# Attention of batches 1 to 7 with the key-value blocks as stationary operand, sums of squares by products with ones, and factors spread through DRAM

## The chip, the cores and the metric

The kernel runs on one core of a Trainium2 chip. The metric is the time of one execution on the device, in microseconds (us). Three runs of the kernel before gave 1651.33, 1654.06 and 1650.82, so the median is 1651.33. All traces are of single profiled executions.

Five engines work side by side, each in the order of its own instructions: PE multiplies matrices (a stationary operand is loaded, a moving one streams past it, the product lands in a bank of PSUM), DVE and ACT work on elements and are the ones that empty PSUM here, POOL does element work in SBUF, SP issues DMAs. They wait for one another by semaphores.

## What is computed

The reference, cut to what matters. All numbers are float32.

```python
# q, k, v: (8 batches, 8 heads, 576 tokens, 64)
kv  = np.einsum('bhsd,bhse->bhde', k, v)
out = np.einsum('bhsd,bhde->bhse', q, kv)
rms = np.sqrt(np.mean(out * out, axis=-1, keepdims=True) + 1e-06)
x   = out / rms * g_norm                 # then heads side by side: x is (4608, 512)
p   = domain_probs / (domain_probs.sum(-1, keepdims=True) + 1e-09)
for e in range(4):                       # w1[e]: 512 x 1024, w2[e]: 1024 x 512
    out += p[:, e:e + 1] * (np.maximum(x @ w1[e], 0.0) @ w2[e])
```

There is no softmax: a head's keys and values shrink to one 64 x 64 block `kv`, and each token's row of q is multiplied by it. The row of 64 that results is divided by its root mean square. The second part multiplies x (and the hidden layer) by the weights of four experts; it is most of the arithmetic.

## The kernel before

**The two parts.** The tokens come in nine chunks of 512: chunk c below 8 is the first 512 tokens of batch c, the ninth holds the last 64 tokens of all batches (`REM`). For every expert e and chunk c there is one step s = 9e + c of products up and down. These use a scheme with seven products for eight blocks at two levels, so their operands are sums and differences of blocks, which DVE and POOL make (`x_forms`, `combine`), and their results are added by DVE (`total` in `up`, line 1370). A product is issued by `halves_of` (line 479) as two halves of 64 columns of the array.

**Attention of batches 1 to 7** (`attention`, lines 956 to 1168) runs beside the products of expert 0: batch c + 1 in step c. It makes x in turned form, features on partitions and tokens along the row, because a product needs x that way. Per batch there are two halves s of four heads (two pairs o, two heads r each):

- q is loaded by eight DMAs and turned in blocks of 32 by DVE (line 1035).
- `key_values`: 20 products make the four 64 x 64 blocks; ACT copies them to SBUF.
- `attend`: blocks of 64 tokens of q are stationary and a 64 x 64 block of kv moves past them, 32 products for the first 512 tokens (line 1088) and 4 for the last 64 (line 1097). The results have tokens on partitions.
- `evacuate` copies them to SBUF. `norm_rows` squares on ACT (line 995), sums over the 64 features on DVE (line 1001), takes the square root on ACT and inverts it with one refining step on 16 columns (`inverse_root`, lines 720 to 739), and multiplies x by the factors (line 1010).
- `turn_x` (line 1129) turns x by eight transposes on PE, and ACT copies them out of PSUM times the gain (line 1138).

The last 64 tokens of both halves are normed together at the end of the batch, turned by two transposes (`turn_left`, line 1150), copied (line 1156) and stored in DRAM in `x_left`.

Batch 0 goes another way (`opening`), which the change leaves alone.

**What sets the order.** Nothing of it is written by hand. `plan.add` takes each operation with a key (its place in steps), a cost in us for each engine that may do it, what it reads and writes, and `kb` for a DMA. `Plan.layout` then lays out the whole program before it is issued: an engine that comes free takes the ready operation that is due first; PE takes the first ready one in the order of keys. A DMA is booked as ending at `max(bus, t + 1.5) + kb / 215 + 0.5`. `port=True` keeps DVE and POOL from working at once on operations that would share a port. For each step, `layout` tries 12 draws (60 for the early steps) of random shifts of the due times, runs the plan a step and 1.3 further, and keeps the draw that leaves PE idle least. The order of each engine is then fixed in the program; on the chip each instruction still waits by semaphores for what it needs.

**PSUM.** There are eight banks: two each of `u1`, `u2` (products up), `db` (products down) and `ab` (products down and attention). A seed is a copy by ACT into a bank on which PE then adds (`op.seed`); it has to lie on columns that PE wrote last, which the loop at the end (lines 1851 to 1857) asserts from `op.marks`.

Of the kernel before, what the change touches and what calls it, by code (L numbers as in the profile page):

```python
# [27 lines left out]
class Op:  # L28
    def __init__(self, key, cost, fn, reads, writes, kb, port):
        self.key, self.cost, self.fn, self.kb, self.port = key, cost, fn, kb, port  # L30
        self.outs = list(writes)
        self.bufs = list(dict.fromkeys(list(reads) + self.outs))
        self.deps = {}
        self.start = self.end = self.eng = None
        self.marks = self.seed = None
        self.early = self.gang = self.opens = False
# [5 lines left out]
class Plan:  # L42
# [18 lines left out]
    TRIES, LOOK, SPREAD = 12, 1.3, 1.5  # L61
# [32 lines left out]
    def layout(self, slots, later, idle, idle_banks, idle_until):  # L94
# [54 lines left out]
        self.order = []  # L149

        steps = {}
        for op in self.ops:
            steps.setdefault(math.floor(op.key), []).append(op)
        for step in sorted(steps):
            begin = self.save()
            tried = []
            for n in range(self.TRIES * (5 if step < 3 else 1)):
                draw = random.Random(100 * n + step)
                for op in steps[step] + steps.get(step + 1, []):
                    op.due = op.base + (draw.gauss(0.0, self.SPREAD) if n else 0.0)  # L160
                if self.run(step + 1 + self.LOOK):
                    tried.append((self.t - self.worked, n))
                self.restore(begin)
            n = min(tried)[1]
            draw = random.Random(100 * n + step)
            for op in steps[step] + steps.get(step + 1, []):
                op.due = op.base + (draw.gauss(0.0, self.SPREAD) if n else 0.0)
# [6 lines left out]
    def save(self):  # L174
# [4 lines left out]
        copied.update({name: dict(getattr(self, name)) for name in ("live", "ended", "missing", "busy")})  # L179
# [31 lines left out]
    def ready(self, op, eng, front):  # L211
# [10 lines left out]
        for k, n in need.items():  # L222
# [7 lines left out]
            if k in self.first and any(o.due < op.due for o in self.first[k] if o is not op):  # L230
                return None
            when = max(when, sorted(free)[n - 1][0])
# [77 lines left out]
    def begin(self, op, eng):  # L310
# [16 lines left out]
        for b in op.outs:  # L327
            if b.kind is not None and b.slot is None:
                free[b.kind].sort()
                b.slot = free[b.kind].pop(0)[1]  # L330
                b.ap = self.slots[b.kind][b.slot]
        for held in list(self.waiting.values()) + list(self.first.values()):
# [27 lines left out]
def kernel(  # L360
# [60 lines left out]
    gcol = const.tile([P, 1], F32, name="gcol")  # L421
    p_all = const.tile([P, NBLK, E], F32, name="p_all")
# [6 lines left out]
        "ss": (2, 2 * H), "rt": (2, 4 * H),  # L429
# [39 lines left out]
    }  # L469
    plan = Plan()  # L470
# [249 lines left out]
    def inverse_root(key, ss, rt, n, count):  # L720
# [7 lines left out]
        def invert(eng):  # L728
            a, r, w = ss.ap[0:n, 0:count], rt.ap[0:n, 0:count], rt.ap[0:n, 2 * H:2 * H + count]
# [226 lines left out]
    def attention(b, key, span, rem):  # L956
# [25 lines left out]
        def norm_rows(key, name, x, squares, count):  # L982

            ss, rt = Buf("ss", f"ss{name}"), Buf("rt", f"rt{name}")
            width = count * D

            def by_head(ap):
                return ap.rearrange("p (b d) -> p b d", d=D)

            for at_ in range(0, width, NT):  # L990
                n = min(width, NT)
                sq = squares or Buf("ab", f"sq{name}_{at_}")
                plan.add(
                    key, act(n),
                    lambda eng, sq=sq, at_=at_, n=n: nc.scalar.activation(
                        out=sq.ap[:, 0:n], in_=x.ap[:, at_:at_ + n], func=ACT.Square),
                    reads=[x], writes=[sq],
                )
                plan.add(
                    key, dve(n),  # L1000
# [892 lines left out]
```

## Time and profile before

| | before |
|---|---|
| median of three runs | 1651.33 us |
| the profiled execution: span from first to last instruction | 1650.8 us |
| PE busy | 1642.3 us, 99% |
| DVE, ACT, POOL busy | 1255.2, 992.5, 737.0 us |
| moved by DMA | 232.48 MB, 141 GB/s mean |
| TensorE clock granted | 0.999 of full speed |

A row of a group names the line, the engine, the operation, what it writes and reads, the shape and the count; then its busy time in us, the mean of one in ns, and the time that the engine stood idle before it, with what ended most of that. A product on PE appears as two MATMUL records, a transpose as one. Records of PE overlap, so what one costs is read from the distance of starts and not from its length. A row of the view of one line or tile has the shortest, median and longest duration in ns. In the order of time, rows of the same kind are merged: start, length, line, count.

### The profile page before, as it was taken

What the parts mean: (1) busy time and instruction counts of PE and PEld (TensorE: products, weight loads), DVE (VectorE), ACT (ScalarE), POOL (GpSimd) and SP (SyncE); (2) the same over time, 40 slices, a digit from 0 to 9 for tenths busy, and PEclk for the clock granted to TensorE, in tenths of its full rate; (3) what the DMA queues carried; (4) which work ended last, traced back from release to release, by engine and by line L of the source; (5) the groups of instructions that cost most, each with busy time, mean ns of one, the idle gap of its engine ahead of it and who ended that gap; (6) DMA issues with size and microseconds to landing.
All of it is one profiled execution on the core that took longest, in us unless ns stands there. A gap on an engine that the chain in (4) does not pass through costs nothing.

```text
span 1650.8 us, 67181 instructions
## 1 busy us (share of the span) xinstructions
PE 1642.3 (99%) x29226; PEld 1566.0 (95%) x29226; DVE 1255.2 (76%) x2198; ACT 992.5 (60%) x2485; POOL 737.0 (45%) x714
## 2 busy tenths in 40 slices
PE   9999999999999999999999999999999999999998
PEld 5688898888999999999999999999999999999996
DVE  4777867777888777887787787777778877777764
ACT  3555665555566666666666666666666566666662
POOL 4545555453443444444354554443354445433341
PEclk9999999999999999999999999999999999999999
DMA  9867556524566444444557444444577544444442
GB/s 235 221 166 212 162 169 173 174 89 148 187 178 158 109 112 124 136 117 116 156 153 183 117 108 116 115 116 115 132 195 164 136 112 117 117 111 111 117 104 52
DMA packets 202704, 232.48 MB, mean 141 GB/s; under 512 B 92778, under 2 KB 142378, under 8 KB 202410
## 3 DMA queue, kind: packets, MB, share of 16 engines
q1 hardware_dynamic: 178858, 191.41, 37.9%
q0 software_dynamic: 23552, 36.78, 14.9%
q8 instruction: 229, 3.75, 0.9%
q14 instruction: 65, 0.53, 0.1%
HBM read 153.95 MB, written 74.19 MB: 138 GB/s over the span
## 4 chain that ended last, share of the span: by engine, by line
PE 99%; DVE 0%; ACT 0%; issue 0%; DMA 0%; POOL 0%; POOLq 0%
PE u L479 48%; PE db L479 32%; PE ab L479 15%; PE ab L1061 1%; PE ab L1088 1%; PE ab L1129 1%; PE ab L1841 0%; PE u L841 0%; PE db L1097 0%; DMA small<-in_q_dram 0%; PE db L880 0%; PE ab L1150 0%; PE ab L900 0%; PE ab L826 0%; DVE small L1035 0%
## 5 line engine op out<-in xcount | busy, mean ns | idle before, releaser
L479 PE MATMUL u<-xf,big 128*64 128x128 f32 x7072 | 513.3, 273 | 0.0
L502 DVE TENSOR_TENSOR big<-big,big 128x1024 f32<-128x1024 f32 (+1 forms) x482 | 448.4, 947 | 26.4 <-ACT big L1326 12.7
L479 PEld LDWEIGHTS u<-xf,big 128*64 128x64 f32 x7072 | 411.6, 137 | 2.7 <-issue 0.8
L479 PE MATMUL db<-big,big 128*64 128x128 f32 (+1 forms) x5144 | 400.2, 292 | 0.4 <-ACT snap L1683 0.4
L479 PE MATMUL u<-xf,w1y 128*64 128x128 f32 x5304 | 396.0, 273 | 0.0
L479 PEld LDWEIGHTS db<-big,big 128*64 128x64 f32 x5144 | 307.3, 137 | 27.8 <-issue 0.8
L1370 DVE TENSOR_TENSOR big<-u,snap 128x256 f32<-128x256 f32 x460 | 192.8, 421 | 176.4 <-PE u L479 130.1
L502 POOL TENSOR_TENSOR big<-big,big 128x256 f32<-128x256 f32 (+1 forms) x176 | 229.6, 1307 | 193.3 <-DVE big L502 98.9
L479 PEld LDWEIGHTS u<-xf,w1y 128*64 128x64 f32 x5304 | 310.7, 137 | 3.0 <-issue 0.5
L1362 ACT ACTIVATE snap<-u 128x256 f32<-128x256 f32 x490 | 187.2, 382 | 174.7 <-PE u L479 146.1
L1362 ACT ACTIVATE big<-u 128x256 f32<-128x256 f32 x460 | 175.4, 383 | 70.3 <-PE u L479 47.2
L502 POOL TENSOR_TENSOR big<-big 128x512 f32<-128x512 f32 (+1 forms) x89 | 109.4, 1230 | 157.6 <-DVE big L502 107.8
L1683 ACT ACTIVATE snap<-db 128x256 f32<-128x256 f32 x252 | 89.0, 353 | 132.4 <-PE db L479 117.8
L1326 ACT ACTIVATE big<-big 128x1024 f32<-128x1024 f32 x128 | 134.5, 1051 | 4.1 <-DVE big L502 2.4
L1691 DVE TENSOR_TENSOR big<-ab,snap 128x256 f32<-128x256 f32 x162 | 68.3, 422 | 66.6 <-ACT snap L1683 39.5
L1534 POOL DMA_DIRECT2D out_dram<-big x116 | 102.7, 1120 | 35.2 <-ACT big L1510 32.2
L1362 ACT ACTIVATE u<-u 128x256 f32<-128x256 f32 x245 | 90.8, 371 | 38.9 <-PE u L479 26.4
L502 DVE TENSOR_TENSOR big<-big 128x512 f32<-128x512 f32 (+1 forms) x125 | 90.2, 728 | 1.4 <-PE db L479 1.4
L479 PE MATMUL ab<-kv,big 128*64 128x128 f32 x1280 | 89.9, 273 | 0.0
L479 PE MATMUL ab<-big,big 128*64 128x128 f32 (+1 forms) x1256 | 89.8, 277 | 0.0
L1510 ACT ACTIVATE big<-big,p_all 128x256 f32<-128x256 f32 x182 | 85.6, 500 | 1.5 <-DVE big L1721 0.7
L1721 POOL TENSOR_TENSOR big<-big 128x512 f32<-128x512 f32 x22 | 28.1, 1278 | 110.1 <-DVE big L502 97.8
(201 smaller groups left out, 2409.4 us busy)
## 6 DMA issues: line engine op xcount, KB each, us to landing
xf<-x SPq DMA_DIRECT2D x104, 512.0 KB, 3.6
xf<-x_h SPq DMA_DIRECT2D x85, 256.0 KB, 3.3
out_dram<-big POOLq DMA_DIRECT2D x80, 256.0 KB, 5.6
xf<-x SPq DMA_DIRECT2D x78, 256.0 KB, 3.6
x<-xf SPq DMA_DIRECT2D x36, 512.0 KB, 3.6
big<-in_moe_w_dram SPq DMA_DIRECT2D x29, 512.0 KB, 7.3
big<-in_moe_w_dram POOLq DMA_DIRECT2D x18, 512.0 KB, 6.2
x_h<-big SPq DMA_DIRECT2D x17, 512.0 KB, 4.8
```

The lines of the kernel that those rows point to most:

```text
L479: nc.tensor.matmul(out_[cols], lhsT=lhsT[:, cols], rhs=rhs, **kw)
L502: lambda eng: adder(eng).tensor_tensor(out=out_(), in0=a(), in1=b(), op=op),
L1061: nc.tensor.matmul(bank.ap[r * D:(r + 1) * D, o * D:(o + 1) * D], lhsT=ks[r], rhs=vs[r], start=(j == 0), stop=(j == len(sets) - 1), skip_g ...
L1088: nc.tensor.matmul(raw[r].ap[c * D:(c + 1) * D, (o * NR + t) * D:(o * NR + t + 1) * D], lhsT=qt.ap[half, col:col + D], rhs=kv.ap[half, o * ...
L1326: lambda eng: nc.scalar.activation(out=b.ap[:], in_=b.ap[:], func=ACT.Relu),
L1362: lambda eng: nc.scalar.activation(out=where(), in_=ps.ap[:, 0:HN], func=ACT.Copy),
L1370: lambda eng: nc.vector.tensor_tensor(out=block(whole, a, t), in0=src.ap[:, 0:HN], in1=add_.ap[:], op=ALU.add),
L1510: lambda eng: nc.scalar.activation(out=cell(i, half), in_=ap(), func=ACT.Copy, scale=prob()),
L1534: nc.gpsimd.dma_start(out=dst, in_=cell(i)[parts, :], accum_op=ALU.add)
L1683: lambda eng: nc.scalar.activation(out=where(), in_=group_of(ps.ap), func=ACT.Copy),
L1691: lambda eng: nc.vector.tensor_tensor(out=cell(tq, dq), in0=group_of(src.ap), in1=group_of(add_.ap), op=ALU.add,),
L1721: lambda eng: adder(eng).tensor_tensor(out=whole(to), in0=whole(a), in1=whole(b), op=ALU.add),
```

## The change

In `attention`, for each half of a batch:

- **q's layout.** The heads of a pair o now lie on one half of the partitions, the head r along the row. The key-value blocks are placed to match, with `key_values` in another order of loops and the same 20 products.
- **`attend`.** A block of kv is stationary and q streams past it: four products of 320 tokens and four of 256. The result has features on partitions and tokens along the row, so x is turned from the start. `turn_x`, `turn_left` and their copies go, and `norm_rows` with them.
- **Sums of squares.** ACT squares x into what will be x's place. `total` multiplies the squares by `ones`, stationary operands of 32 columns that hold ones for one head each: eight products of 128 columns and four of 32, in four strips of 32 partitions of one bank. So each head's sum over its 64 features stands in a row.
- **The factors.** Root and inversion work on 160 columns (`root`, `invert`, the same refining step). A DMA stores the rows that matter in DRAM (`roots`), two DMAs (`spread`) bring each head's factors back on all 64 partitions of its features, and two more do so for the last 64 tokens (`spread_left`). DVE then multiplies x, gain and factors in one instruction, and in a second for the last tokens.
- The last tokens of a batch are stored in `x_left` from there.

In the planner, the draws of each step are no longer tried but written down (`DEALS`, with a spread of 1, 2 or 4 by the draw's number), also for the steps after attention. `written` tells how many columns of a bank PE wrote last, and a seed (`wants`) takes a bank with enough of them. `sides`, which holds the ones, is set by three memsets on POOL.

The diff, cut to its core:

```diff
-    TRIES, LOOK, SPREAD = 12, 1.3, 1.5
+    SPREADS = 1.0, 2.0, 4.0
+    DEALS = {
+        -2: 25, -1: 39, 0: 49, 1: 28, 2: 72, 3: 8, 5: 18, 6: 22, 7: 12, 8: 22, 9: 17, 10: 9, 11: 22, 12: 28,
+        13: 4, 14: 5, 17: 5, 18: 3, 19: 1, 20: 5, 21: 4, 26: 4, 27: 4, 28: 1, 29: 2, 35: 2
+    }
...
+    def deal(self, step, n):
+
+        draw = random.Random(100 * n + step)
+        for op in self.steps[step] + self.steps.get(step + 1, []):
+            op.due = op.base + (draw.gauss(0.0, self.SPREADS[n % 3]) if n else 0.0)
...
+            if op.wants:
+                free = [f for f in free if self.written.get((k, f[1]), 0) >= op.wants]
+                if not free:
+                    return None
...
+    sides = const.tile([P, 48], F32, name="sides")
+    ones = [sides[:, 16:48], sides[:, 0:32]]
...
             def key_values(eng, bank=kbank, held=held):
+                sets = [list(zip(rows_of(kt), rows_of(vt))) for kt, vt in held]
+                for j in range(len(sets[0])):
+                    for r in range(2):
+                        for o in range(2):
+                            ks, vs = sets[o][j]
                             nc.tensor.matmul(
+                                bank.ap[o * D:(o + 1) * D, r * D:(r + 1) * D],
+                                lhsT=ks[r], rhs=vs[r], start=(j == r == 0),
+                                stop=(j == len(sets[0]) - 1), skip_group_check=True,
                             )
...
+            def attend(eng, raw=raw, rest=rest, kv=kv, qt=qt):
+                for at_, width, to in ((0, FIRST, raw), (FIRST, S - FIRST, rest)):
+                    for r in range(2):
+                        for o in range(2):
+                            half, cols = slice(o * D, (o + 1) * D), slice(r * D, (r + 1) * D)
+                            nc.tensor.matmul(
+                                to[o].ap[cols, 0:width], lhsT=kv.ap[half, cols],
+                                rhs=qt.ap[half, r * S + at_:r * S + at_ + width],
+                            )
+            plan.add(
+                at(2 * s + 1.0), {"PE": 1.1}, attend, reads=[qt, kv], writes=raw + rest,
+                early=True, gang=True,
+            ).wide = {**{b: FIRST for b in raw}, **{b: S - FIRST for b in rest}}
...
+            plan.add(
+                when, act(2 * NT),
+                lambda eng, qt=qt, xh=xh: nc.scalar.activation(
+                    out=two(xh.ap[:]), in_=tokens(qt.ap, False), func=ACT.Square),
+                reads=[qt], writes=[xh],
+            )
...
+            def total(eng, ss=ss, xh=xh, s=s):
                 for o in range(2):
+                    for j in range(NR):
                         nc.tensor.matmul(
+                            ss.ap[j * R:(j + 1) * R, 0:P], lhsT=ones[o],
+                            rhs=xh.ap[:, (2 * j + o) * P:(2 * j + o + 1) * P],
+                            start=(o == 0), stop=(o == 1), skip_group_check=True,
                         )
+                for j in range(NR):
+                    nc.tensor.matmul(
+                        ss.ap[j * R:(j + 1) * R, P:P + GR], lhsT=ones[0],
+                        rhs=xs.ap[:, s * P + j * GR:s * P + (j + 1) * GR],
+                        start=False, stop=True, skip_group_check=True,
+                    )
+            plan.add(
+                when, {"PE": 0.75}, total, reads=[xh, xs], writes=[ss]).wide = {ss: P + GR}
...
+            def invert(eng, ss=ss, xh=xh, n=wide):
+                w, r = xh.ap[:, 0:n], xh.ap[:, n:2 * n]
+                nc.vector.reciprocal(out=r, in_=r)
+                nc.vector.scalar_tensor_tensor(
+                    out=w, in0=ss.ap[:, 0:n], scalar=D * EPS, in1=r, op0=ALU.add, op1=ALU.mult)
+                nc.vector.scalar_tensor_tensor(
+                    out=w, in0=w, scalar=-0.5 / D, in1=r, op0=ALU.mult, op1=ALU.mult)
+                return nc.vector.scalar_tensor_tensor(
+                    out=w, in0=w, scalar=1.5, in1=r, op0=ALU.add, op1=ALU.mult)
+
+            plan.add(when, act(wide), root, reads=[ss], writes=[xh])
+            plan.add(
+                when, {"DVE": 0.65 + 0.0044 * wide}, invert, reads=[ss, xh], writes=[xh], port=True)
+            sent, kept_at = Buf(None, f"root{n}"), roots[b, s]
+            plan.add(
+                when, SPC,
+                lambda eng, xh=xh, to=kept_at, n=wide: nc.sync.dma_start(
+                    out=to[:].rearrange("r n t -> n r t"), in_=xh.ap[0:P:8, 0:n]),
+                reads=[xh], writes=[sent], kb=10,
+            )
+            def spread(eng, xh=xh, src=kept_at):
+                for r in range(2):
+                    nc.sync.dma_start(
+                        out=xh.ap[r * D:(r + 1) * D, :].rearrange("p (n t) -> p n t", t=P),
+                        in_=src[r, :, 0:P].unsqueeze(0).to_broadcast([D, 8, P]))
+            def spread_left(eng, src=kept_at, mine=mine):
+                for r in range(2):
+                    nc.sync.dma_start(
+                        out=xs.ap[r * D:(r + 1) * D, mine].rearrange("p (n t) -> p n t", t=GR),
+                        in_=src[r, 0::2, P:].unsqueeze(0).to_broadcast([D, NR, GR]))
+            plan.add(when, {"SP": 1.1}, spread, reads=[sent], writes=[xh], kb=520)
+            plan.add(when, {"SP": 1.1}, spread_left, reads=[sent], parts=[xs], kb=100)
             when = at(2 * s + 2.2)
+            plan.add(
+                when, dve(2 * NT),
+                lambda eng, xh=xh, qt=qt: nc.vector.scalar_tensor_tensor(
+                    out=two(xh.ap[:]), in0=tokens(qt.ap, False), scalar=gcol[:], in1=two(xh.ap[:]),
+                    op0=ALU.mult, op1=ALU.mult),
+                reads=[qt, xh], writes=[xh], port=True,
+            )
...
                 if mm == 1:
                     seeds = [copy(bank[2], lambda b=bank[2]: b.ap[:, 0:HN])]
+                    seeds[0].wants = HN
```

More of the change, by code (lines that the diff above doesn't have):

```diff
@@ L468 @@
         for c in range(NCH) for m in ("h0", "h1", 1, 2, 3, 4, 5, 6, 7)
+    }
+    roots = {
+        (b, s): dram.tile([2, 8, P + REM // 2], F32, tag=f"roots{b}_{s}", name=f"roots{b}_{s}")
+        for b in range(1, B) for s in range(2)
     }
@@ new lines, in attention @@
+            rest = [Buf("db", f"rest{n}_{o}") for o in range(2)]
+            def attend(eng, raw=raw, rest=rest, kv=kv, qt=qt):
[7 more added lines that the diff above has]
+                            )
@@ new lines, in tokens @@
+            def tokens(ap, left, qt=qt):
+                return ap[:, 0:2 * S].rearrange("p (o t) -> p o t", o=2)[
+                    :, :, NT if left else 0:S if left else NT]
+            mine = slice(s * P, (s + 1) * P)
+            plan.add(
[5 more added lines that the diff above has]
+            plan.add(
+                when, act(P),
+                lambda eng, qt=qt, mine=mine: nc.scalar.activation(
+                    out=two(xs.ap[:, mine]), in_=tokens(qt.ap, True), func=ACT.Square),
+                reads=[qt], parts=[xs],
+            )
```

189 lines of the change are left out of this document (53 added, 136 removed).

## The prediction

> **What bounds the kernel now.** I read the page's head first, then PE's waits, then the stage in which batches 1 to 7 go through attention.
>
> ```profile
> span 1650.8 us, 67181 instructions
> PE 1642.3 (99%) x29226; PEld 1566.0 (95%) x29226; DVE 1255.2 (76%) x2198; ACT 992.5 (60%) x2485; POOL 737.0 (45%) x714
> PE 99%; DVE 0%; ACT 0%; issue 0%; DMA 0%; POOL 0%; POOLq 0%
> ```
>
> The chain that ended last is PE for 99% of its length. A busy PE need not be PE at its peak, so the next question is whether PE ever waits. PE's waits of the whole run:
>
> ```profile
> PE ab L1841 <- POOL ident masks.py:199: 1.4, 1, 1.4
> PE ab L900 <- DVE big L775: 0.9, 2, 0.8
> PE u L479 <- DVE big L1370: 0.6, 1, 0.6
> PE ab L1088 <- issue: 0.5, 1, 0.5
> PE db L479 <- ACT snap L1683: 0.4, 1, 0.4
> ```
>
> They come to 3.8 us. So a better order of the same work can bring at most about 2.4 us (the 1.4 us for the identity at the start stays), and everything else must come from PE doing less. Batches 1 to 7 go through attention up to about 360 us (the scaling L1010, whose row stands below, runs from 53 to 356); busy time there, in stretches of 41 us (columns: PE, PE's weight loads, DVE, ACT, POOL, then PE's clock, the DMA engines' share, GB/s):
>
> ```profile
> 82.00:123.00 41.00, 40.55 (x752) 36.35 (x748) 30.43 (x63) 23.57 (x60) 20.15 (x19) 1.00 0.66 172
> 123.00:164.00 41.00, 40.89 (x670) 34.51 (x668) 30.44 (x65) 24.10 (x61) 23.14 (x23) 1.00 0.77 213
> 164.00:205.00 41.00, 40.93 (x736) 35.10 (x732) 33.33 (x67) 25.32 (x62) 20.12 (x22) 1.00 0.57 158
> ...
> sum 287.00, PE 286.37 PEld 250.68 DVE 215.62 ACT 171.47 POOL 146.87; mean PE 40.91 PEld 35.81 DVE 30.80 ACT 24.50 POOL 20.98
> ```
>
> PE is full at full clock, DVE is busy for 30.8 of 41, ACT for 24.5. The time of the change is therefore PE's balance plus whatever new waits reach PE.
>
> **PE's prices.** Two pieces of the chain give what a record of a plain product costs (one fp32 product is two records):
>
> ```profile
> 339.67 3.45 PE db L479 x32
> 390.97 1.75 PE u L479 x32
> ```
>
> A record of 128 columns takes 1.75/32 = 0.0547 us, one of 256 columns 3.45/32 = 0.1078: time goes by columns, 0.421 ns each, with nearly nothing per record. These products run as two column halves of 64, two at a time. Now the attention step and what surrounds it, in order of time (start, length, line, count):
>
> ```profile
> 176.85 0.66 PE L479 MATMUL u<-big,w1y 128*64 128x128 f32 x8
> 177.44 1.16 PE L1088 MATMUL ab<-kv,small 64*64 64x64 f32 x64
> 178.42 0.40 PE L1097 MATMUL db<-kv,small 64*64 64x64 f32 x8
> 178.75 0.66 PE L479 MATMUL u<-xf,w1y 128*64 128x128 f32 x8
> 179.24 0.61 PE L479 MATMUL u<-xf,big 128*64 128x128 f32 x8
> ```
>
> From 176.85 to 179.24 are 2.39 us, of which 16 plain records are 0.875. Attention costs 1.515. Inside it, 64 records of 64 columns take 0.98 (177.44 to 178.42), 0.239 ns a column: four quadrants of the array at a time, nearly twice the rate of two halves. Change of tile shape costs too: the eight records before L1088 last 0.59 instead of 0.4375, so 0.15 to enter. And the turning back of x:
>
> ```profile
> 200.62 2.11 PE L479 MATMUL db<-big,big 128*64 128x256 f32 x18
> 202.67 0.44 PE L1150 MATMUL ab<-ident,snap 128*128 128x128 f32 x2
> 203.03 0.66 PE L479 MATMUL u<-small,big 128*64 128x128 f32 x8
> 203.52 0.61 PE L479 MATMUL u<-big,w1y 128*64 128x128 f32 x8
> 204.06 1.09 PE L1129 MATMUL ab<-ident,small 128*128 128x128 f32 x8
> 205.08 0.66 PE L479 MATMUL u<-xf,big 128*64 128x128 f32 x8
> 205.57 1.68 PE L479 MATMUL db<-big,big 128*64 128x256 f32 x14
> ```
>
> L1129 with its shape changes costs 205.57 - 203.52 - 2 x 0.4375 = 1.175 us a half, L1150 203.52 - 200.62 - 18 x 0.1078 - 0.4375 = 0.52 us a batch.
>
> **The change part by part, on PE.** (a) The transposes go: 2 x 1.175 + 0.52 = 2.87 us a batch. (b) Attention has the same columns (64 x 64 + 8 x 64 = 4608 before, 8 x 320 + 8 x 256 = 4608 after) in 16 long records, its tiles in the same rotation of four quadrants. At half of 0.421 they take 0.97, at 0.239 they take 1.10; 0.15 to enter and some 0.15 to leave stay. I take 1.3, a gain of 0.2 a half (0.1 to 0.25). (c) The key-value products keep their count and their alternation of two column halves: nothing. (d) New: the products with ones. 8 products of 128 columns and 4 of 32 make 16 x 128 + 8 x 32 = 2304 columns, each product in a strip of 32 columns of the array, four strips in turn. No row shows strips of 32. By four at a time, as in L1088, they take 0.49 to 0.55, with 0.3 for the shape changes 0.8; two at a time 0.97 + 0.3 = 1.27; one at a time 1.94 + 0.3 = 2.24. I take 0.8: the nearest row is L1088, where four tiles that share no part of the array run together, and four strips share none either.
>
> In a sentence apart: the Trainium skill ("TensorE: Matmul & The Clock Gate", Part 3, Measured speedup vs the span model) has three strips of 32 run 2.38 times as fast as one, not three; four strips at that efficiency would be about 3.2 times, an estimate that makes (d) 0.9 and the whole 1.4 us dearer.
>
> PE's balance is -1.175 - 0.2 + 0.8 = -0.575 a half, -1.15 - 0.52 = -1.67 a batch, over seven batches **-11.7 us**. With two strips at a time it is -5.1, with one +8.5.
>
> **The change on the other engines.** Rows for it:
>
> ```profile
> L540 DVE RECIPROCAL inv<-tot x2: 178/266/353, 52.9 to 124.2; 128x4 f32<-128x4 f32 x1, 128x32 f32<-128x32 f32 x1
> L735 DVE SCALAR_TENSOR_TENSOR rt<-rt x26: 157/174/176, 13.5 to 356.1; 128x16 f32<-128x16 f32 x14, 128x4 f32<-128x4 f32 x7, 128x8 f32<-128x8 f32 x4, 64x8 f32<-64x8 f32 x1
> L1010 DVE TENSOR_TENSOR small<-small,rt x14: 1214/1218/3162, 53.2 to 356.2; 128x1024 f32<-128x1024 f32 x14
> L1001 DVE TENSOR_REDUCE ss<-ab 128x8 f32<-128x512 f32 x28 | 18.5, 686 | 5.1 <-ACT ab L995 4.9
> L995 ACT ACTIVATE ab<-small 128x512 f32<-128x512 f32 x28 | 15.9, 594 | 0.1
> L1138 ACT ACTIVATE big<-ab,gcol 128x512 f32<-128x512 f32 x28 | 18.3, 683 | 2.9 <-PE ab L1129 2.6
> L1326 ACT ACTIVATE big<-big 128x1024 f32<-128x1024 f32 x128 | 134.5, 1051 | 4.1 <-DVE big L502 2.4
> 183.69 3.16 DVE L1010 TENSOR_TENSOR small<-small,rt 128x1024 f32<-128x1024 f32 x1
> ```
>
> ACT loses 2 x 0.594 and 2 x 0.683 a half and gains one square of 1024 (1.05, as L1326) and one of 128 (about 0.3): 1.2 us less. DVE loses two reductions (1.37) and the scaling (1.22) and gains a multiply of 1024 with the gain (1.2 to 1.4) and one of 128 (about 0.3). Its inversion grows from 16 columns to 160. The reciprocal goes from 178 ns at 4 columns to 353 at 32, 6.25 ns a column, so 178 + 156 x 6.25 = 1150 ns at 160; three more instructions at about 320 (174 and some 1 ns a column) make 2.1 us. The planner books 0.65 + 0.0044 x 160 = 1.35, so DVE runs about 0.8 us late each half.
>
> Behind the inversion on DVE stand the sums that empty PE's banks (L1370), so lateness there can stop PE. How much is covered? At 183.69 the scaling took 3.16 instead of 1.22, 1.94 us late, and no wait of PE in the list above came of it. So I price the 14 inversions at 1.5 us together, between 0 and 14 x 0.8 = 11. DVE as a whole has no more to do than before.
>
> DMA: a half gains one store of 10 KB and four spreads, two of 256 KB and two of 32 KB, in rows of 512 and 128 bytes. Rows from 82 to 371 us, KB each and us to landing:
>
> ```profile
> x<-xf SPq DMA_DIRECT2D x22, 512.0 KB, 4.1
> small<-in_q_dram SPq DMA_DIRECT2D x80, 72.0 KB, 2.5
> kv<-in_v_dram SPq DMA_DIRECT2D x20, 48.0 KB, 4.3
> x_left<-snap SPq DMA_DIRECT2D x6, 128.0 KB, 2.3
> L508 SPq DMA_DIRECT2D small<-in_q_dram x95: 312/496/1835, 59.8 to 315.4; - x95
> ```
>
> A store lands in about 2.3, a spread in about 4.1, the way through DRAM takes some 6.4 us; the planner books 2.05 and 4.4, so it agrees. Some 1.15 MB more a batch are 28 GB/s in a stage that moves 158 to 213. SP issues ten more DMAs a batch, about 5 us. The spreads wait on SP for the store; behind them stand loads of the next q, k and v and stores of x. The code asks for q 0.3 of a chunk of 41 us ahead, so those have some 12 us. The wait for the spread stands before DVE's multiply, and behind that the same sums as above. The planner puts other work of PE there. I cost the way through DRAM at nothing as long as it lands when booked; uncovered it is the slower rival below. Three memsets on POOL come after the identity that ends PE's first wait. In the stages after 360 us nothing is left to gain or, with the same products, to lose; the draws set for them change only an order.
>
> Sum against the profiled execution: 1650.8 - 11.7 + 1.5 = 1640.6. The median of the runs, 1651.33, is 0.5 above that span, so **1641 us**.
>
> **The rivals.** (1) *The inversion is not covered*: every 0.8 us reaches PE, 11 instead of 1.5, **1651**. For it: DVE is the busiest engine after PE. Against: the 1.94 us that cost nothing. (2) *Strips of 32 run two at a time*: **1648**; one at a time: **1661**. Against: quadrants are independent in L1088. For: no row shows strips. (3) *Slower: DVE held by a late spread.* DVE takes instructions in order, and its multiply waits for a DMA that cannot be asked for early. About 1.9 us are covered; beyond that each us late costs 14. It decides from 1.9 + 10.2/14 = 2.6 us late in every half; at 3.7 late the loss is 14 x 1.8 = 25, **1666**. For: 48 KB of v land after 4.3 us where 128 KB alone take 2.3, so a queue of 2 us is usual. Against: the DMA engines are busy for 0.57 to 0.77, and q's loads come after 2.5. (4) *The new draws also remove the waits that are left and the inversions are covered*: 1641 - 1.5 - 2.4, **1637**. That the change doesn't do what it says would show as transposes left in the trace; the diff takes them all out.
>
> **How the numbers follow.** Forecast 0.58, (4) 0.10, two strips 0.08, (1) 0.10, (3) 0.09, one strip 0.05. About 0.2% (3.3 us) is what a measurement tells from no change. Faster are the forecast, (4) and two strips, 0.76; the same is (1), 0.10; slower (3) and one strip, 0.14. The range leaves out the 0.14 and little else: 1636, below (4), to 1653, above (1).
>
> **What would show it.** Right: no L1129 or L1150 and about 1.3 us less of them and of attention a half; ones products at 0.8 us with their shape changes, four starting together; the reciprocal of 160 columns at about 1.15 us; PE's waits still under 5 us. Wrong: ones products spaced one after another; DVE's multiply idle until a DMA, with PE waiting for a sum behind it; PE's idle time in 82 to 369 above 10 us.

## The result and the profile after

| | before | after |
|---|---|---|
| median | 1651.21 us (1650.82 to 1654.06) | 1645.14 us (1644.02 to 1645.75) |
| profiled span | 1650.8 us | 1644.0 us |
| PE busy | 1642.3 us | 1632.1 us |
| DVE, ACT, POOL busy | 1255.2, 992.5, 737.0 us | 1285.5, 972.8, 687.0 us |

The ratio is 0.9954 (95%: 0.994 to 0.9968): 6.1 us faster, by spans 6.8. Forecast were 10, in a range that holds the result. The head of the page of the changed kernel, its chain, and then PE's waits (us in total, times, the longest):

```profile
span 1644.0 us, 66026 instructions
PE 97%; DMA 1%; DVE 1%; SPq 0%; issue 0%; ACT 0%; DVEq 0%
```

```profile
PE ab L1866 <- POOL ident masks.py:199: 1.4, 1, 1.4
PE db L501 <- ACT snap L1707: 1.2, 1, 1.2
PE u L501 <- DVE big L1173: 0.9, 1, 0.9
...
PE ab L1050 <- DMA kv<-in_v_dram: 0.6, 1, 0.6
PE db L501 <- DVE big L1715: 0.6, 1, 0.6
PE u L501 <- DVE big L1393: 0.5, 1, 0.5
```

The chain is no longer PE alone. PE's waits come to 7.2 us, where they were 3.8, and there are two new names among them: the multiply with the factors (L1173) and values that land late (`in_v_dram`). A copy out of PSUM behind DVE (L1707) stood in the list before too, as L1683 with 0.4; it has grown to 1.2.

**PE's work** is read in the order of time (start, length, line, count), at two places of one batch, after:

```profile
148.90 0.61 PE L501 MATMUL u<-xf,big 128*64 128x128 f32 x8
149.43 0.77 PE L1075 MATMUL ab<-small,kv 64*64 64x320 f32 x8
150.02 0.61 PE L1075 MATMUL db<-small,kv 64*64 64x256 f32 x8
150.56 0.66 PE L501 MATMUL u<-xf,w1y 128*64 128x128 f32 x8
151.05 1.04 PE L501 MATMUL u<-xf,big 128*64 128x128 f32 x16
...
153.24 0.61 PE L501 MATMUL u<-xf,w1y 128*64 128x128 f32 x8
153.77 0.64 PE L1115 MATMUL ab<-big,sides 128*32 128x128 f32 x16
154.23 0.24 PE L1121 MATMUL ab<-snap,sides 128*32 128x32 f32 x8
154.41 1.09 PE L501 MATMUL db<-w2y,big 128*64 128x128 f32 x16
155.33 1.04 PE L501 MATMUL db<-big,big 128*64 128x128 f32 x16
```

From 148.90 to 151.05 are 2.15 us, of which 16 plain records are 16 x 0.0547 = 0.875: attention costs 1.28 (1.3 was put, 1.515 read before). From 153.24 to 155.33 are 2.09; less 24 plain records, 1.31, the products with ones cost **0.78** (0.8 was put). Their 16 records of 128 columns take 0.46, or 0.225 ns a column, where the four quadrants of L1088 took 0.239: four strips of 32 run together as fully as four quadrants, and the products start in fours, 6 to 7 ns apart. The transposes are gone. So PE's balance is -1.175 - 0.235 + 0.78 = -0.63 at this place; with the median over all halves of attention before (1.474 instead of 1.515) and of the ones (0.785) it is -0.58 a half, and 14 x -0.58 - 7 x 0.52 is **-11.8 us**. -11.7 was put.

The Trainium skill ("TensorE: Matmul & The Clock Gate", Part 3, Measured speedup vs the span model) has three strips at 2.38 times one, which made these products 0.9 by estimate. The trace does not bear the estimate out: 0.78.

So 11.8 us came off PE as counted, the span fell by 6.8, and **5.0 us are missing**, where 1.5 had been put for waits. The 5.0 is a difference, not a reading: the list of waits grew by 3.4 only. But the list counts from the end that is modelled for the record before, so it is short. By the distance of starts the wait of 1.16 us at 115.81 below is 1.33 and that of 0.61 at 274.51 is 0.83; counted so, the waits of the whole run grew by about 4 to 4.5 us. Nearly all of what is missing is therefore PE waiting. Where DVE and POOL stand in the stage of attention, in the same seven stretches of 41 us as before (sum and mean):

```profile
sum 287.00, PE 283.39 PEld 247.33 DVE 232.74 ACT 159.30 POOL 105.63; mean PE 40.48 PEld 35.33 DVE 33.25 ACT 22.76 POOL 15.09
```

DVE went from 215.6 to 232.7, POOL from 146.9 to 105.6. The groups of lines in 82 to 369 us tell why: sums of operands moved from POOL to DVE. Of the kernel before, then of after:

```profile
L502 DVE TENSOR_TENSOR big<-big,big 128x1024 f32<-128x1024 f32 (+1 forms) x57 | 53.6, 950 | 2.1 <-PE db L479 1.0 <-ACT big L1326 0.8
L502 POOL TENSOR_TENSOR big<-big,big 128x1024 f32<-128x1024 f32 (+1 forms) x38 | 68.6, 1807 | 33.2 <-DVE big L502 13.7 <-DVE snap L1010 5.5 <-PE db L479 3.6
```

```profile
L524 DVE TENSOR_TENSOR big<-big,big 128x1024 f32<-128x1024 f32 (+1 forms) x62 | 68.9, 1123 | 3.0 <-PE db L501 1.5 <-POOL xf L524 0.4
L524 POOL TENSOR_TENSOR big<-big,big 128x1024 f32<-128x1024 f32 (+1 forms) x32 | 52.2, 1637 | 44.2 <-DVE big L524 15.1 <-DVE xf L524 7.9 <-DMA small<-in_q_dram 4.1
```

This group alone gave DVE 15.3 us more and POOL 16.4 less: of sums of 1024 columns, 45 instead of 34 ran on DVE. The prices of the single operations are as put (rows of the lines: shortest, median, longest in ns):

```profile
L1137 DVE RECIPROCAL big<-big x14: 1136/1149/1153, 50.3 to 360.1; 128x160 f32<-128x160 f32 x14
L1140 DVE SCALAR_TENSOR_TENSOR big<-big x14: 324/325/326, 52.0 to 361.6; 128x160 f32<-128x160 f32 x14
L1173 DVE SCALAR_TENSOR_TENSOR big<-small,gcol,big x14: 1272/1278/1743, 61.0 to 369.3; 128x1024 f32<-128x1024 f32 x14
```

1149 ns (1150 were put) and three times 325 make an inversion of 2.12 us, 0.77 over the booked 1.35.

**Where PE waits now.** The first of two places, in the order of time, all engines:

```profile
108.33 1.14 DVE L1137 RECIPROCAL big<-big 128x160 f32<-128x160 f32 x1
...
110.72 2.37 POOL L524 TENSOR_TENSOR big<-big,big 128x1024 f32<-128x1024 f32 x1 [4.13 <-DMA small<-in_q_dram]
...
111.64 0.42 DVE L1393 TENSOR_TENSOR big<-u,snap 128x256 f32<-128x256 f32 x1 [0.76 <-PE u L501]
111.98 1.38 DVE L1542 SCALAR_TENSOR_TENSOR big<-big,p_all,big 128x256 f32<-128x256 f32 x1
...
113.29 2.35 DVE L524 TENSOR_TENSOR big<-big,big 128x1024 f32<-128x1024 f32 x2
...
114.53 1.06 ACT L1349 ACTIVATE big<-big 128x1024 f32<-128x1024 f32 x1 [0.76 <-DVE big L524]
115.50 0.26 ACT L1707 ACTIVATE snap<-db 128x128 f32<-128x128 f32 x1
...
115.81 0.66 PE L501 MATMUL db<-big,big 128*64 128x128 f32 x8 [1.16 <-ACT snap L1707]
```

The inversion ends at 110.54. DVE itself makes up the time: at 111.64 it has stood idle for PE for 0.76 us. What stays late is POOL: its sum of 2.37 us starts only 0.18 us after the inversion's last instruction. The profile of the changed kernel names a DMA there; in one of the same kernel taken later, the row names the inversion (L1142):

```profile
109.55 2.37 POOL L524 TENSOR_TENSOR big<-big,big 128x1024 f32<-128x1024 f32 x1 [4.12 <-DVE big L1142]
```

While POOL adds, L1542 on DVE takes 1.38 instead of its median of 0.478, so 0.9 more, and makes the sum for ACT's relu late; ACT's copy L1707 stands behind that relu, and PE, which needs the bank, waits 1.16 us. The second place:

```profile
264.53 1.28 SPq L1158 DMA_DIRECT2D big<-roots  x2
265.86 1.29 SPq L1164 DMA_DIRECT2D snap<-roots  x2
267.20 0.61 SPq L530 DMA_DIRECT2D kv<-in_k_dram  x1
267.85 0.91 SPq L530 DMA_DIRECT2D kv<-in_v_dram  x2
...
269.54 1.28 DVE L1173 SCALAR_TENSOR_TENSOR big<-small,gcol,big 128x1024 f32<-128x1024 f32 x1 [1.87 <-DMA kv<-in_k_dram]
269.77 2.26 SPq L530 DMA_DIRECT2D kv<-in_v_dram  x2
...
271.21 0.66 PE L501 MATMUL u<-big,w1y 128*64 128x128 f32 x8 [0.54 <-DVE big L1393]
...
274.51 1.32 PE L1050 MATMUL ab<-kv 120*64 120x64 f32 x37 [0.61 <-DMA kv<-in_v_dram]
```

The spreads are issued at 264.53 and DVE's multiply starts 5.0 us later, after 1.87 us in which DVE did nothing (the DMA named is the last that the profile can put there). The sum L1393 stands behind it and PE waits 0.54: 1.33 of the 1.87 were covered. And the loads of k and v stand on SP behind the four spreads, 2.6 us of issuing, so the last of v comes late and PE waits a second time, 0.61. The largest wait in the list behind the multiply (0.9) is at a third place, 79.56. SP itself is held as well; the largest of its waits in 41 to 371 us:

```profile
SPq L1151 <- DVE big L1142: 37.2, 11, 15.5
```

L1151 is the store of the roots: SP stood 37.2 us before it until the inversion was done, with later loads behind it. SP waits in the kernel before too, for buffers to come free, so the sum alone proves nothing; the two waits above are where it shows.

### The profile page after: what moved, and what is told of

Its sections match the earlier page's. It is cut to its first block, busy times and chain, and to the rows that moved or that the text cites. A ratio compares the mean times of both kernels' runs of the same rounds, so it can differ in the third digit from the quotient of the medians.

```text
span 1644.0 us, 66026 instructions
## 1 busy us (share of the span) xinstructions
PE 1632.1 (99%) x28652; PEld 1551.9 (94%) x28652; DVE 1285.5 (78%) x2191; ACT 972.8 (59%) x2436; POOL 687.0 (42%) x668
## 4 chain that ended last, share of the span: by engine, by line
PE 97%; DMA 1%; DVE 1%; SPq 0%; issue 0%; ACT 0%; DVEq 0%
PE u L501 48%; PE db L501 31%; PE ab L501 15%; PE ab L1050 1%; DMA kv<-in_v_dram 1%; PE ab L1075 0%; PE ab L1115 0%; DMA big<-in_v_dram 0%; PE db L1075 0%; DMA big<-roots 0%; SPq L530 0%; DVE big L524 0%; DVE big L1173 0%; PE db L902 0%; PE u L863 0%; DMA kv<-in_k_dram 0%
## 5 line engine op out<-in xcount | busy, mean ns | idle before, releaser
L524 DVE TENSOR_TENSOR big<-big,big 128x1024 f32<-128x1024 f32 (+1 forms) x552 | 517.8, 956 | 25.5 <-ACT big L1349 9.8
L501 PE MATMUL u<-xf,big 128*64 128x128 f32 x6496 | 473.6, 273 | 0.0
L501 PE MATMUL db<-big,big 128*64 128x128 f32 (+1 forms) x5328 | 407.5, 292 | 2.0 <-ACT snap L1707 1.2
L501 PEld LDWEIGHTS u<-xf,big 128*64 128x64 f32 x6496 | 378.7, 137 | 3.4 <-issue 0.8
L501 PEld LDWEIGHTS db<-big,big 128*64 128x64 f32 x5328 | 316.9, 137 | 29.8 <-ACT snap L1707 1.4
L1393 DVE TENSOR_TENSOR big<-u,snap 128x256 f32<-128x256 f32 x462 | 193.3, 420 | 161.6 <-PE u L501 120.4
L524 POOL TENSOR_TENSOR big<-big,big 128x256 f32<-128x256 f32 (+1 forms) x169 | 204.4, 1212 | 214.0 <-DVE big L524 89.4
L1707 ACT ACTIVATE snap<-db 128x256 f32<-128x256 f32 x252 | 89.0, 354 | 128.9 <-PE db L501 116.9
L1349 ACT ACTIVATE big<-big 128x1024 f32<-128x1024 f32 x134 | 140.9, 1051 | 7.8 <-DVE big L524 7.8
L1715 DVE TENSOR_TENSOR big<-ab,snap 128x256 f32<-128x256 f32 x174 | 73.2, 420 | 59.7 <-ACT snap L1707 39.2
L524 DVE TENSOR_TENSOR big<-big 128x512 f32<-128x512 f32 (+1 forms) x137 | 102.0, 750 | 1.7 <-POOL big L524 1.1
L1746 POOL TENSOR_TENSOR big<-big 128x512 f32<-128x512 f32 x26 | 33.1, 1274 | 145.9 <-DVE big L524 143.1
```

Source lines behind the costliest of these rows:

```text
L501: nc.tensor.matmul(out_[cols], lhsT=lhsT[:, cols], rhs=rhs, **kw)
L524: lambda eng: adder(eng).tensor_tensor(out=out_(), in0=a(), in1=b(), op=op),
L1349: lambda eng: nc.scalar.activation(out=b.ap[:], in_=b.ap[:], func=ACT.Relu),
L1393: lambda eng: nc.vector.tensor_tensor(out=block(whole, a, t), in0=src.ap[:, 0:HN], in1=add_.ap[:], op=ALU.add),
L1707: lambda eng: nc.scalar.activation(out=where(), in_=group_of(ps.ap), func=ACT.Copy),
L1715: lambda eng: nc.vector.tensor_tensor(out=cell(tq, dq), in0=group_of(src.ap), in1=group_of(add_.ap), op=ALU.add,),
```

## The experiments

Two theories stood against each other. One: the inversion of 160 columns is late on DVE. The other: the way through DRAM holds DVE or SP. Besides, the draws came new with the change and could have brought or taken anything. Gains below are each kernel's median against the kernel before, run beside it. The changed kernel gained 6.1 the first time and 6.6 when it was measured again, so differences from it are given as a range.

**The inversion without its division** (same order of all instructions; the factors are then not the right ones):

```diff
-                nc.vector.reciprocal(out=r, in_=r)
+                nc.vector.tensor_copy(out=r, in_=r)
```

> The changed kernel in the same order, with the reciprocal of 160 columns (1.15 us in its trace, where the planner books some 0.3) replaced by a copy, so the inversion's result is left out. If the new waits come from the mis-booked inversion (14 halves, each some 0.85 us late on DVE), they fall by 2 to 4 us: about 1642. If they come from the way through DRAM or from the order itself, the time stays within 1 us of the changed kernel's 1645.1.

Measured: 1642.62, ratio 0.9943 (0.993 to 0.9955), a gain of 8.8 instead of 6.1. The line's row:

```profile
L1137 DVE COPY big<-big x14: 225/239/244, 49.8 to 356.9; 128x160 f32<-128x160 f32 x14
```

14 x 0.91 = 12.7 us off DVE gave 2.2 to 2.7 on PE.

**No way back from DRAM**: the 56 spreads are left out, so the factors in x are not the right ones; the order stays.

```diff
             def spread(eng):
-                for r in range(2):
-                    nc.sync.dma_start(...)
+                return None
```

> The changed kernel in the same order, with the four spreads of each half left out (56 DMAs; the factors do not arrive, the store stays, DVE's multiply has nothing of DMA to wait for, SP issues less). If late spreads and the loads queued behind them on SP make the new waits, about 3 us go (in the profile of the changed kernel 0.7 at 271 us behind a multiply held by a spread, 0.9 at 274 us behind a late load of v, 1.6 at 78 us behind the multiply): about 1642. If the inversion or the order makes them, it stays within 1 us of 1645.1.

Measured: 1642.30, ratio 0.994 (0.9926 to 0.9954), a gain of 9.1: 2.5 to 3.0 more than the changed kernel. So this way isn't free either.

**Both at once:**

> The changed kernel in the same order with both left out, the division (a copy in its place) and the four spreads of each half. Alone they gave 2.5 and 2.8 us. If the two waits lie at different places, they add up: 1639.8, which is the time before less PE's balance of 11.7, so nothing would be left to explain. If both pay for one and the same crowding of DVE, it stays at 1641.5 to 1642.3.

Measured: 1641.35, ratio 0.9935 (0.9923 to 0.9948), a gain of 10.4. The two give 2.5 and 2.8 alone and 4.1 together (against 6.35, the mean gain of the changed kernel's two measurements): some 1.1 us are shared, with about half a us of noise on it. One shared place is the wait behind the multiply at 271 (0.5): it is gone without the division and 0.3 without the spreads. Which wait belongs to which, PE's lists show. Without the spreads:

```profile
PE db L501 <- ACT snap L1701: 1.2, 1, 1.2
```

The wait at 115.8 (the copy, here L1701) is unchanged; that for v is gone from the list. Without the division, v's is the largest after the identity, and the copy's has fallen to 0.4:

```profile
PE ab L1050 <- DMA kv<-in_v_dram: 0.9, 1, 0.9
PE db L501 <- ACT snap L1707: 0.4, 1, 0.4
```

There POOL's sum starts 0.18 us after the inversion too, but earlier against DVE, and L1542 takes 0.62. So the first place is the inversion's, through POOL's sum, and the wait for v the spreads'. With both left out, the waits are 5.0 us against 3.8 in the kernel before; of what is left over, a sum (L1709, 0.6 at 115.7) and a multiply (L1167, 0.5 at 78.8) stand in the lists of the runs before it as well. About half a us of the third place is therefore neither the division's nor the spreads'.

**One reciprocal instead of root and refining step:**

```diff
-            def invert(eng, ss=ss, xh=xh, n=wide):
...
+            def invert(eng, xh=xh, n=wide):
+                return nc.vector.reciprocal(out=xh.ap[:, 0:n], in_=xh.ap[:, n:2 * n])
```

It takes the root's reciprocal as it is, without the refining step.

> The changed kernel in the same order, with the inversion cut to the reciprocal alone: the refining step (three instructions of some 0.33 us on 160 columns) is left out. DVE's inversion then takes 1.15 us, less than the 1.35 booked. If the mis-booking is what costs, the gain is that of the run without division, about 2.5 us: 1642 to 1643, with the factors still computed. If the division itself did something else, such as holding the port shared with POOL, less comes of it: 1644 to 1645.

Measured: 1642.39, ratio 0.994 (0.9927 to 0.9952). Three instructions less (0.975 us) gave what a shorter first one (0.91 us) gave: when the inversion ends counts, not which of its instructions has the time. Once more, beside the changed kernel on the same chip:

> The changed kernel once more, unaltered, beside the others on one chip: 1644 to 1646. Its profile shows whether the waits at 76, 114 to 118 and 271 to 274 us stand at the same places; those that come from the order of work should stay within 0.1 us, those that hang on when a DMA lands should move.

> The run with the plain reciprocal once more, beside the changed kernel on the same chip. If the refining step's three instructions cost what the first pair of runs says, it is 2 to 3.5 us faster than the changed kernel: 1641 to 1643.

The changed kernel took 1644.78 (1644.09 to 1645.98), ratio 0.9958 (0.9946 to 0.9969). In its list the copy's 1.2 and a sum's 0.6 (L1715) came again to within 0.1; of what hangs on DMAs, v's went from 0.6 to 0.7 and the multiply's at the third place from 0.9 to 0.5, and the wait for L1393 behind a held multiply is now 0.6 at 168 us instead of 0.5 at 271. So the first place belongs to the order, and the places at which a DMA is late shift from profile to profile. The plain reciprocal took 1642.26 (1641.86 to 1643.51), ratio 0.9942 (0.993 to 0.9953). The runs don't overlap: 2.5 us. This version beats both kernels. PE's waits of it that answer the rows above:

```profile
PE ab L1050 <- DMA kv<-in_v_dram: 0.5, 1, 0.5
PE db L501 <- ACT snap L1700: 0.3, 1, 0.3
```

The copy's wait is down as it is without the division, and POOL's sum holds L1542 for no time here (0.48). The wait for v is not so steady: in the first profile of this version it was 2.0. That it hangs on the spreads is shown by the runs without them; its size is not.

**The draws of before's rule.** The best of 12 draws a step (60 for the early ones) at spread 1.5, written down for the changed kernel:

```diff
-    SPREADS = 1.0, 2.0, 4.0
-    DEALS = {-2: 25, -1: 39, 0: 49, 1: 28, 2: 72, ...}
+    SPREADS = 1.5, 1.5, 1.5
+    DEALS = {-1: 51, 0: 54, 1: 20, 2: 15, 3: 2, ...}
```

> The new attention with the draws that the procedure of the kernel before picks (12 draws a step, 60 in the early ones, shifts of 1.5) in place of the written ones. If the written draws carry part of the gain, it is slower than the changed kernel by 3 us or more, 1648 to 1652, little or no faster than before. If the new waits hang on the inversion and the DMAs alone, the order of the rest matters little: 1644 to 1647.

Measured: 1649.94, ratio 0.999 (0.9981 to 0.9998), a gain of 1.5. The same attention in another order of the same work keeps a quarter of the gain. Its largest wait is for DVE's sums (L1390), 2.0 us in five times; after 369 us, where attention is over, PE waits 1.0 instead of 0.4.

**Wide draws for the kernel before** (75 a step, spreads 1, 2 and 4, picked by the planner's idle time):

> The kernel before with its attention untouched and draws picked from 75 a step with shifts of 1, 2 and 4, the procedure of the changed kernel's kind. If the draws alone bring something, it is faster than before by 1 to 2 us (at most the 2.4 us of waits that a better order can remove): 1649 to 1650. If the gain is attention's alone, it stays at 1651.2.

Measured: 1654.71, ratio 1.0015 (1.0006 to 1.0024), 3.3 us slower than the kernel before: a miss, as a gain of 1 to 2 was expected. One wait takes most of it:

```profile
PE ab L1060 <- DMA kv<-in_v_dram: 2.5, 1, 2.5
```

A draw that the planner likes can ask for v too late for the chip. More draws are no gain in themselves.

**The spreads written beside x**, to an unused tile in DRAM, to keep their issue on SP and take away what DVE waits for; the factors in x are then not the right ones.

```diff
-                        out=xh.ap[r * D:(r + 1) * D, :]...
+                        out=away[r * D:(r + 1) * D, :]...
```

> The changed kernel in the same order, with the four spreads of each half written to an unused place in DRAM instead of x's place, so DVE's multiply waits for no DMA (and has no factors), while SP issues them and they wait for the store as before. If it was DVE held by late spreads that cost 2.8 us, the gain stays: about 1642.5. If it was SP, where loads of k and v stand behind the spreads, or the traffic, the gain goes: 1644 to 1645.

Measured: 1661.40, ratio 1.006 (1.0047 to 1.0072). It doesn't tell what it was made for: all spreads write one tile, so each waits on SP for the one before to land (42.6 us in 24 times between 41 and 371 us, the largest of its waits there), and the loads behind them come late.

```profile
PE ab L1051 <- DMA kv<-in_v_dram: 10.2, 6, 2.6
```

It does show that what holds SP reaches PE, through v.

**The spreads issued by POOL**, with the plain reciprocal (`nc.gpsimd.dma_start` in place of `nc.sync.dma_start`):

> The plain reciprocal, with the four spreads of each half issued by POOL in place of SP; the order of PE, DVE and ACT is unchanged. If loads of k and v are late because they stand behind the spreads on SP, PE's waits for them go (2.2 us at 270 us in the first profile of the plain reciprocal) and the time falls to 1640 to 1642. If DVE then waits longer for POOL's share of the sums, or for spreads that POOL issues late, it is slower than the plain reciprocal: 1643 to 1648.

Measured: 1646.78, ratio 0.9971 (0.996 to 0.9982), 4.5 us slower than with SP. A spread lands after 4.8 us in the median, as with SP (4.7), but one took 8.5. The wait for v is gone from PE's list though the same bytes move, which speaks for the place on SP and not for the traffic. In the order of time:

```profile
271.05 1.28 DVE L1166 SCALAR_TENSOR_TENSOR big<-small,gcol,big 128x1024 f32<-128x1024 f32 x1 [3.13 <-issue]
272.25 0.42 DVE L1386 TENSOR_TENSOR big<-u,snap 128x256 f32<-128x256 f32 x1
...
272.72 0.66 PE L501 MATMUL u<-big,w1y 128*64 128x128 f32 x8 [1.80 <-DVE big L1386]
```

The multiply was held 3.13 us (the profile names no releaser), PE waited 1.80: again 1.33 covered. Beyond the cover, a late factor cost one for one at these two places.

**Without `port=True`** on the inversion and the multiplies, draws made anew:

```diff
-                when, {"DVE": 0.65 + 0.0044 * wide}, invert, reads=[ss, xh], writes=[xh], port=True)
+                when, {"DVE": 0.65 + 0.0044 * wide}, invert, reads=[ss, xh], writes=[xh])
```

> The new attention with its inversion and its multiplies no longer booked as holding the port that DVE and POOL share, so the planner may run POOL beside them; draws picked anew, 75 a step. In the changed kernel POOL is busy for 132 of the first 369 us (184 before) and DVE for 289 (265 before). If the port booking pushes the sums from POOL to DVE, POOL comes back to 155 or more, DVE falls to 280 or less, and PE's waits between 41 and 123 us (4.6 in the changed kernel, by the distance of starts) fall below 3.5. If the crowding comes from elsewhere, they stay above 4. The total is uncertain by the draws, some 3 us: 1641 to 1648.

Measured: 1656.48, ratio 1.0027 (1.0017 to 1.0037). A miss: 1641 to 1648 were expected. The part on the sums came as expected: POOL is busy for 154.3 of the first 369 us and DVE for 273.4, and PE stands idle for 1.6 us between 41 and 123 us where it was 3.1. But between 123 and 369 us PE stands idle for 9.2 where it was 1.4. The sum of the seven stretches, and the row of the small multiply:

```profile
sum 287.00, PE 277.25 PEld 237.19 DVE 218.76 ACT 152.60 POOL 121.80; mean PE 39.61 PEld 33.88 DVE 31.25 ACT 21.80 POOL 17.40
```

```profile
L1177 DVE SCALAR_TENSOR_TENSOR snap<-small,gcol,snap x14: 340/532/2457, 63.1 to 384.0; 128x128 f32<-128x128 f32 x14
```

The multiply of 128 columns took 532 ns in the median and up to 2457; with the port booked (L1180 of the changed kernel) its median was 342 and its longest 348. All seven slow ones began while POOL was at a sum and ended 0.15 us after it. DVE was also held longer by DMAs in this order, and the granted clock was 0.96 in two of the seven stretches, which by estimate is 0.04 x 82 = 3.3 us. So how much of the loss is the port, how much the draws and how much the clock stays open.

**The inversion booked at its measured time**, draws made anew:

```diff
-                when, {"DVE": 0.65 + 0.0044 * wide}, invert, ...
+                when, {"DVE": 2.1}, invert, ...
```

> The changed kernel with its inversion booked at 2.1 us, what it takes, and draws picked anew for that (110 a step, the best of four rounds). If the wrong booking is the cause of the waits, a right one removes them as taking the work away does: 1642 to 1643. If what counts is the load on DVE and the luck of the draws, it gains nothing: 1645 to 1655.

Measured: 1648.33, ratio 0.9977 (0.9968 to 0.9987), 3.5 us slower than the changed kernel beside it. Its largest waits are for a DMA (L1047, 2.0) and for the multiply (L1170, 1.3). A right price in the planner with other draws is worth less than the draws that were written down; what it would bring with the same draws, no run shows.

## Why the prediction was right in direction and 4 us off

The measured 1645.14 lies 4 us above the forecast, within the range of 1636 to 1653. That alone says little: the range is 17 us wide, and 1637, 1648 and 1651, the times of three rivals, lie in it too. What counts is whether the terms of the sum were right.

**PE's balance was right**, term by term: transposes -1.175 and -0.52 as read, attention -0.19 to -0.235 (-0.2 put), ones 0.78 (0.8 put), together -11.8 (-11.7 put). Taking the strips' rate from the quadrants was the right row, and both rivals of slower strips fell. The expectation of four starting together holds too.

**The term for the waits was mis-sized: 1.5 us were put, 5.0 came back.** It failed in three of its steps.

- "I cost the way through DRAM at nothing as long as it lands when booked." Leaving the spreads out gained 2.5 to 3.0. It mostly does land in time, but the four DMAs are 2.6 us of SP's time a half, the store before them holds SP until the inversion is done, and the loads of k and v behind come late; once DVE's multiply waits 1.87 us for the landing, too. The text gave a cover for q's loads only, 12 us, and none for v's.
- "DVE as a whole has no more to do than before." Only its new operations had been added up. But the largest group of sums grew by 15.3 us on DVE and shrank by 16.4 on POOL; without `port=True` POOL's total came back from 105.6 to 121.8, so the booking of the port goes with some 16 of the 41 us that POOL lost, in a run that had other draws as well. An inversion late by 0.77 then meets a fuller engine. At 2.5 us for 12.7 us of DVE's time, 14 x 0.77 late would cost 2.1: an estimate from the first experiment, near the 1.5 put. The path was not the one put either: at the place that was followed, DVE itself caught up and the lateness reached PE through POOL's sum, which held L1542.
- "A better order of the same work can bring at most about 2.4 us", and, of the stages after 360 us, that the draws "change only an order" with nothing to lose. The bound holds for what an order can bring to the kernel before. For what an order can cost it said nothing, and other draws cost 3.3 us on the kernel before and 4.6 on the changed one, 0.6 of that as waits after 369 us.

With division and spreads both out the gain is 10.4 of the 11.8. The waits of that run, 5.0 against 3.8, account for 1.2 of the last 1.4: mostly the sum and the multiply named there (0.6 and 0.5). Why these two stay is open.

**The rivals.** That every late inversion reaches PE (1651) was wrong by about five times: on average over the 14 inversions, one us of DVE's time is worth 0.2 of PE's. Rival (3), DVE held by a late spread, occurs as it was described, with 1.33 covered where 1.9 was put, but in three halves of the changed kernel, by 0.3, 0.3 and 1.9 us, not in all 14. Rival (4) went the other way: the new order has more waits, not fewer. The sign that was named for a wrong forecast, PE's idle time above 10 us in 82 to 369, didn't come (287.00 - 283.39 = 3.6). Another, DVE's multiply idle until a DMA with PE waiting for a sum behind it, came once, at 269.54 and 271.21. And PE's waits, which should have stayed under 5, came to 7.2.

**Open:** how much of the 6.1 us is the attention and how much the written draws. With draws by one rule for both (the best of 12 or 60) the change brought 1.5; with wide draws for the kernel before and the written ones after, 9.4. The plan is drawn anew whenever an operation changes, so the two cannot be parted with one pair of runs.

## What to carry to other kernels

On a kernel whose PE is full, what comes off PE could be counted here to a few per cent from the distance of starts, but the gain is that less the new waits, and those follow the load of the engine that empties PSUM: add up what the planner will move onto it, not only the new operations. A result that goes through DRAM is paid for on the queue that issues it, by the loads that stand behind. Where the order is drawn, run the old kernel under new draws and the new one under old before crediting the change.

## What the runs showed that was not expected

- After some waits PE runs slower for a while, and the length of the wait alone doesn't decide which. In the kernel without `port=True`, PE stood for 1.97 us at 271.7 to 273.6, and in stretches of 4 us the granted clock (third figure from the end) was:

```profile
272.00:276.00 4.00, 2.37 (x24) 2.37 (x26) 3.52 (x6) 0.26 (x2) 0.74 (x2) 0.73 0.91 197
276.00:280.00 4.00, 4.00 (x66) 4.00 (x64) 2.62 (x4) 1.71 (x6) 4.00 (x4) 0.85 1.07 343
```

The 16 records that start at 273.63 took 1.62 us instead of 0.875. The clock fell in the same run after a wait of 1.44 us at 174.8 too. But the kernel before with wide draws waited 2.45 us, from 76.53 to 78.98, and kept its clock:

```profile
78.00:82.00 4.00, 3.02 (x110) 2.81 (x112) 1.04 (x4) 1.12 (x4) 1.15 (x2) 1.00 1.04 402
```

What decides is not shown here.

- DVE operations on two operands in SBUF are held while POOL adds: L1542 took up to 1452 ns with a median of 478, and all 8 that were slow began while POOL was at a sum and ended 0.28 us after it. The same line with one operand in PSUM stays between 436 and 486 ns, also where POOL adds beside it. L1140, two operands in SBUF as well but kept apart from POOL by the plan, stays between 324 and 326. The Trainium skill ("SBUF — State Buffer", SBUF: two separate sides) has the pair of ports taken by one instruction as a whole, with the other blocked; 111.98 to 113.36 above, beside POOL's 110.72 to 113.09, agrees.
